# A linear-attention and MLP kernel: chunks 8 to 23 computed by blocks of 64 tokens with the state on the key rows, the powers of w in one table, and a new order

## The chip, the cores and the metric

The kernel runs on one core of a Trainium2 chip. A core has a matrix engine (TensorE, here PE, with its weight loads PEld), a vector engine (DVE), a scalar engine (ACT), GpSimd (POOL) and a queue that issues the DMAs (SP). Each engine takes its instructions in program order and waits for the others by semaphores. The metric is device time in microseconds; the kernel before takes 511.69 us (median of 3 runs, 511.52 to 512.78).

## The reference

Attention with a decaying state for 4 batches, 8 heads, 768 tokens and 48 dimensions per head; its output goes through an MLP (384 to 2048 and back).

```python
for t in range(S):                      # 768 tokens
    cur = einsum('bhd,bhe->bhde', u*k[t], v[t])
    y[t] = einsum('bhd,bhde->bhe', r[t], state + cur)
    state = w * state + einsum('bhd,bhe->bhde', k[t], v[t])
x = y as (3072 tokens, 384)
h = x @ w_in;  sp = log(1 + exp(h))
return (h * erf(sp)) @ w_out
```

## The kernel before

**Chunks.** The 768 tokens are cut into 6 steps of 128; with 4 batches that makes 24 chunks, and chunk g follows chunk g-4 of its own batch. Within a chunk the recurrence is a product: r is scaled by w^i and k by w^-j (steps R and K, tables `wr` and `wk`), A = k^T r is a 128x128 matrix for each head (step A, line 307, matmuls of 48 rows by 64 columns of weights), everything above the diagonal is masked away by a predicated copy into `am` (step P), whose diagonal came from u (steps Q and M). Step Y (line 339) adds two products into one PSUM bank: v with `am`, and the state `sbd` with the scaled r. Step D (line 358) makes the chunk's own contribution to the state, S adds it (line 372) and multiplies by w^128 (line 376). For chunks 8 to 23, half of the A matmuls leave out the 64 columns that the mask drops anyhow, and the predicated copy is made of three pieces. X (lines 379, 382) splits y into a high and a low part, x. D is left out for the last four chunks.

**The MLP.** Four chunks make one block x of 512 tokens. For each of 96 units n (6 blocks by 16 groups of 128 hidden rows) step f (line 405) makes 9 matmuls of 512 columns into `h`, steps a, b, z, c, d, e, g, h, l apply the activation on ACT and DVE (l, the low half `gl`, on DVE or POOL), and step p (line 464) makes 9 matmuls into three accumulators. O copies them out. The weights are split into high and low halves at the start (steps F and C, lines 125 to 137).

**Start and end.** The powers of w are made by doubling on DVE, a square, a reciprocal and a product at a time (lines 175 to 187), from w, with two pairs of tables (`wre`, `wke` for chunks 0 to 3, `wr`, `wk` for the others). Dummy matmuls (W, line 94) fill PE. At the very end step Z counts the heads whose w lies out of a range (a tiny matmul, line 512, and a reduce, line 513); every engine loads the count (line 514) and branches on it (line 596) past a slower version.

**What sets the order.** A string ORDER lists the steps, and each engine gets its instructions in that order; `+` sends a step to POOL, `*` to ACT, none to DVE, and `@` names a PSUM bank. Nothing else schedules them.

```python
L405  nc.tensor.matmul(out=h, lhsT=w[:, f, q, :], rhs=x[:, xi, q, :], ...)   # step f, 9 of them
L464  nc.tensor.matmul(out=acc[e], lhsT=w[:, f, es], rhs=g, ...)             # step p, 9 of them
```

Of the kernel before, what the change touches and what calls it, by code (L numbers as in the profile page):

```python
# [26 lines left out]
P = 128  # L27
C = 128
# [8 lines left out]
V0, K0, R0, AW = 1024, 1472, 1856, 2240  # L37
B0 = AW - 512
# [3 lines left out]
def body(ctx: ExitStack, tc: tile.TileContext, att, early, wcol, u, win, wout, levels, outT):  # L42
# [20 lines left out]
    chunks = {}  # L63


    def load_a(g):
        chunks[g] = (xp if g == 3 else apool).tile([P, AW], F32, tag="x" if g == 3 else "att", name=f"att{g}")
        nc.sync.dma_start(out=chunks[g][:, 0:V0], in_=att[g, :, 0:V0])

    def load_b(g):  # L70
        t = chunks[g]
        if g < 4:
# [68 lines left out]
    pw = fp.tile([PR, 2, NPAIR, C // 2], F32, tag="gh", name="pw")  # L141
    nc.gpsimd.memset(pw[:, 0, :, 0:1], 1.0)
    uq = const.tile([PR, NPAIR, 32], F32, name="uq")
# [31 lines left out]
    nc.vector.tensor_scalar(out=wp[:, 0, 0], in0=wc, scalar1=0.7, scalar2=0.97, op0=ALU.max, op1=ALU.min)  # L175
    for n in range(7):
        m = 1 << n
        nc.vector.tensor_tensor(out=wp[:, n + 1, 0], in0=wp[:, n, 0], in1=wp[:, n, 0], op=ALU.mult)
        nc.vector.reciprocal(out=wp[:, n, 1], in_=wp[:, n, 0])
        if n == 0:  # L180
            nc.vector.tensor_copy(out=pw[:, 1, :, 0], in_=wp[:, 0, 1])
        if n < 6:
            nc.vector.tensor_tensor(out=pw[:, :, :, m:2 * m], in0=pw[:, :, :, 0:m],
                                    in1=wp[:, n, :, :, None].to_broadcast([PR, 2, NPAIR, m]), op=ALU.mult)
    nc.vector.reciprocal(out=wp[:, 7, 1], in_=wp[:, 7, 0])
    for c0, n in ((0, 7), (H, 6)):
        nc.vector.tensor_tensor(out=wke[:, :, c0:c0 + H], in0=pw[:, 1],
                                in1=wp[:, n, 0, :, None].to_broadcast([PR, NPAIR, H]), op=ALU.mult)
        for p in range(NPAIR):
            nc.scalar.mul(out=wre[:, p, c0:c0 + H], in_=pw[:, 0, p], mul=wp[:, n, 1, p:p + 1])  # L190
    for o, i in ((wk, 1), (wr, 0)):
        nc.scalar.copy(out=o[:, :, 0:H], in_=pw[:, i])
        nc.gpsimd.tensor_tensor(out=o[:, :, H:C], in0=pw[:, i],
                                in1=wp[:, 6, i, :, None].to_broadcast([PR, NPAIR, H]), op=ALU.mult)
    for hh in range(2):
        r = slice(64 * hh, 64 * hh + D)
        nc.gpsimd.tensor_tensor(out=uq[r, :, hh], in0=uc[r], in1=wp[r, 0, 0], op=ALU.mult)
# [19 lines left out]

    def prep_k(g, eng):
        t = chunks[g][:PR, 512:V0]
        eng.tensor_tensor(out=t, in0=t, in1=(wke if g < 4 else wk).rearrange("p a c -> p (a c)"), op=ALU.mult)  # L220

    def prep_r(g, eng):
        t = chunks[g][:PR, 0:512]
        eng.tensor_tensor(out=t, in0=t, in1=(wre if g < 4 else wr).rearrange("p a c -> p (a c)"), op=ALU.mult)  # L224

    def prep_n(g, eng):
        t = chunks[g][:, K0:R0]
        eng.tensor_tensor(out=t, in0=t, in1=wkn.rearrange("p a b d -> p (a b d)"), op=ALU.mult)
# [27 lines left out]
    def turn_k(g):  # L256
        tp = bank("h" if g < 4 else "A1", [P, NPAIR, PR], f"kt{g}")
# [11 lines left out]
    def diag_a(t, eng):  # L269
        eng.tensor_tensor(out=t[:, R0:AW], in0=t[:, R0:AW], in1=ub, op=ALU.mult)  # L270

    def diag_b(t, eng):
        eng.tensor_tensor(out=t[:, R0:AW], in0=t[:, R0:AW], in1=t[:, K0:R0], op=ALU.mult)

    def diag_c(t, g):
        q = a2.tile([P, NPAIR, 2], F32, tag="q", name=f"q{g}")
        nc.vector.tensor_reduce(out=q, in_=t[:, R0:AW].rearrange("p (a b d) -> p a b d", b=2, d=D), axis=AX.X,  # L277
# [19 lines left out]
    def a_step(g, tags):  # L297
# [3 lines left out]
        for p in range(NPAIR):  # L301
            for c0, i0 in ((0, 0), (H, H)):
                for hh in range(2):
                    r = slice(64 * hh, 64 * hh + D)
                    jc = c0 if g < 4 else abs(c0 - H * ((hh + p) % 2))
                    i = 0 if g < FULL else i0
                    nc.tensor.matmul(out=ap[hh][jc:jc + H, p, i:C], lhsT=t[r, 512 + p * C + c0:512 + p * C + c0 + H],  # L307
                                     rhs=t[r, p * C + i:(p + 1) * C], start=True, stop=True)
        st_[g]["ap"] = ap

    def predicated(g, am, ap, m, hh):
        if g < FULL:
            nc.vector.copy_predicated(out=by_pair(am), data=by_pair(ap), mask=straight(m) if g < 4 else turned(m, hh))  # L313
            return
        for r, ps, t, c in ((slice(0, P), slice(0, NPAIR), None, slice(H, C)),
                            (slice(0, H), slice(hh, NPAIR, 2), 0, slice(0, H)),
                            (slice(H, P), slice(1 - hh, NPAIR, 2), 1, slice(0, H))):
            if t is None:
                nc.vector.copy_predicated(out=by_pair(am)[:, :, :, c], data=by_pair(ap)[:, :, :, c],
                                          mask=turned(m, hh)[:, :, :, c])  # L320
            else:
                nc.vector.copy_predicated(out=am[r, ps, c], data=ap[r, ps, c],
                                          mask=m[r, t:t + 1, c].to_broadcast([H, NPAIR // 2, H]))
# [38 lines left out]
    def s_views(b, hh):  # L362
        r = slice(64 * hh, 64 * hh + D)
        return r, sbd[r, b, :, D * hh:D * (hh + 1)], wp[r, 7, 0, :, None].to_broadcast([D, NPAIR, D])

    def s_add(g, hh, eng):
        r, sv, w128 = s_views(g % 4, hh)
        ds = st_[g]["ds"]
        if g < 4:
            (nc.scalar.copy if eng is nc.scalar else nc.vector.tensor_copy)(out=sv, in_=ds[r])  # L370
# [135 lines left out]

    def count_bad():

        bad = const.tile([PR, NPAIR], F32, name="bad")
        nc.vector.tensor_tensor(out=bad, in0=wp[:, 0, 0], in1=wc, op=ALU.not_equal)  # L510
# [9 lines left out]
    for i, x in enumerate(words):  # L520
# [11 lines left out]
        elif what == "N" and eng is nc.scalar:  # L532
            copy_k(num)
        elif what in preps:
            preps[what](num, eng)
        elif what == "L":
            (load_a if sub == "a" else load_b)(num)
        elif what == "U":
            load_u()
        elif what == "T":  # L540
            across(wk)
        elif what == "V":
            turn_k(num)
        elif what == "Z":
            rv = count_bad()
        elif what == "Q":
            st_.setdefault(num, {})
            if sub == "a":
                diag_a(chunks[num], eng)
            elif sub == "b":  # L550
                diag_b(chunks[num], eng)
            else:
                st_[num]["q"] = copy_q(num, eng) if num < 4 else diag_c(chunks[num], num)
# [4 lines left out]
        elif what == "H":  # L558
            turn_q(num)
        elif what == "M":  # L560
            st_[num // 10]["am", num % 10] = diag_m(st_[num // 10]["q"], num // 10, num % 10, eng)
        elif what == "A":
            st_.setdefault(num, {})
            a_step(num, [BANKS[c] for c in where or "01"])
        elif what == "P":
# [261 lines left out]
```

## Time and profile before

| what | value |
|---|---|
| time, median of 3 runs | 511.69 us |
| profiled execution, first to last instruction (span) | 508.9 us |
| TensorE clock granted, mean over the span | 0.996 |
| busy: PE, DVE, ACT, POOL | 493.1, 338.1, 403.3, 183.1 us |
| PE h L405 and PE acc L464 on the chain that ended last | 38% and 36% |
| PE y L339, PE A L307, PE ds L358 on it | 6%, 3%, 1% |
| DMA, mean | 93 GB/s |

The profile is of one execution; no device time of that execution is listed beside its span, and the median of the runs lies 2.8 us above it. A matmul's end is modelled, so two matmuls that follow each other overlap in the records: how fast PE goes is read from the starts. A row with xN merges N records; an fp32 matmul leaves two records.

### The profile page before, as it was taken

What the parts mean: (1) busy time and instruction counts of PE and PEld (TensorE: products, weight loads), DVE (VectorE), ACT (ScalarE), POOL (GpSimd) and SP (SyncE); (2) the same over time, 40 slices, a digit from 0 to 9 for tenths busy, and PEclk for the clock granted to TensorE, in tenths of its full rate; (3) what the DMA queues carried; (4) which work ended last, traced back from release to release, by engine and by line L of the source; (5) the groups of instructions that cost most, each with busy time, mean ns of one, the idle gap of its engine ahead of it and who ended that gap; (6) DMA issues with size and microseconds to landing.
All of it is one profiled execution on the core that took longest, in us unless ns stands there. A gap on an engine that the chain in (4) does not pass through costs nothing.

```text
span 508.9 us, 10505 instructions
## 1 busy us (share of the span) xinstructions
PE 493.1 (97%) x4176; PEld 389.5 (77%) x4176; DVE 338.1 (66%) x610; ACT 403.3 (79%) x747; POOL 183.1 (36%) x167
## 2 busy tenths in 40 slices
PE   7789999999999999999999999999999999999994
PEld 3567777877877777787878888787888888878883
DVE  7999999898876956765868644646556453353442
ACT  4788999999997666778776777878778777987982
POOL 6657335433265544625354033513312221202110
PEclk9999999999999999999999999999999999999998
DMA  8656343613605151250131350020120000000001
GB/s 309 222 215 247 123 154 125 216 62 116 243 23 182 64 166 50 90 190 13 51 134 43 105 190 0 7 87 1 63 91 0 1 2 0 33 31 1 0 1 68
DMA packets 14007, 47.34 MB, mean 93 GB/s; under 512 B 1664, under 2 KB 2560, under 8 KB 13952
## 3 DMA queue, kind: packets, MB, share of 16 engines
q1 hardware_dynamic: 13952, 46.61, 26.7%
q8 instruction: 35, 0.57, 0.5%
q14 instruction: 20, 0.16, 0.1%
HBM read 40.31 MB, written 6.29 MB: 92 GB/s over the span
## 4 chain that ended last, share of the span: by engine, by line
PE 86%; DVE 8%; ACT 2%; DMA 1%; issue 1%; POOL 1%; DVEq 0%; ACTq 0%; POOLq 0%
PE h L405 38%; PE acc L464 36%; PE y L339 6%; PE A L307 3%; PE ds L358 1%; DVE s L421 1%; DVE am L313 1%; DMA out_dram<-o 1%; DVE att L220 1%; DMA o<-part 1%; DVE wt L129 1%; DVE gl L448 1%; ACT gh L443 0%; DVE att L224 0%; DVE s L437 0%
## 5 line engine op out<-in xcount | busy, mean ns | idle before, releaser
L405 PE MATMUL h<-x,wih 128*128 128x512 f32 x576 | 183.1, 399 | 1.4 <-DVE s L437 1.0
L448 POOL TENSOR_TENSOR gl<-s,gh 128x512 fp32r<-128x512 f32 x52 | 69.0, 1328 | 213.9 <-ACT gh L443 186.6
L405 PEld LDWEIGHTS h<-x,wih 128*128 128x128 f32 x576 | 106.7, 188 | 28.3 <-DVE s L437 1.9
L464 PE MATMUL acc<-gh,woh 128*128 128x512 f32 x288 | 115.0, 399 | 0.0
L464 PE MATMUL acc<-gl,woh 128*128 128x512 f32 x288 | 114.1, 396 | 0.2 <-DVE gl L448 0.2
L405 PE MATMUL h<-x,wil 128*128 128x512 f32 x288 | 113.7, 395 | 0.0
L464 PE MATMUL acc<-gh,wol 128*128 128x512 f32 x288 | 113.7, 395 | 0.0
L437 DVE SCALAR_TENSOR_TENSOR s<-s,h 128x512 f32<-128x512 f32 x96 | 65.6, 685 | 61.4 <-ACT s L433 61.1
L421 DVE SCALAR_TENSOR_TENSOR s<-s,h 128x512 f32<-128x512 f32 x96 | 65.7, 686 | 59.3 <-ACT s L416 42.4
L425 ACT ACTIVATE s<-s 128x512 f32<-128x512 f32 x96 | 60.2, 628 | 37.3 <-DVE s L421 37.3
L443 ACT CAST gh<-s 128x512 fp32r<-128x512 f32 x96 | 58.7, 614 | 21.6 <-DVE s L437 16.0
L412 ACT ACTIVATE s<-h 128x512 f32<-128x512 f32 x96 | 56.7, 592 | 15.6 <-PE h L405 15.1
L464 PEld LDWEIGHTS acc<-gl,woh 128*128 128x128 f32 x288 | 54.2, 188 | 14.0 <-DVE gl L448 1.5
L464 PEld LDWEIGHTS acc<-gh,woh 128*128 128x128 f32 x288 | 54.1, 188 | 13.4 <-ACT gh L443 0.2
L405 PEld LDWEIGHTS h<-x,wil 128*128 128x128 f32 x288 | 54.1, 188 | 12.9
L464 PEld LDWEIGHTS acc<-gh,wol 128*128 128x128 f32 x288 | 54.2, 188 | 12.7
L416 ACT ACTIVATE s<-s 128x512 f32<-128x512 f32 x96 | 60.4, 632 | 2.1
L433 ACT ACTIVATE s<-s 128x512 f32<-128x512 f32 x96 | 60.3, 629 | 2.1
L429 ACT ACTIVATE s<-s 128x512 f32<-128x512 f32 x96 | 60.4, 629 | 1.9
L448 DVE TENSOR_TENSOR gl<-s,gh 128x512 fp32r<-128x512 f32 x44 | 31.6, 719 | 13.7 <-ACT gh L443 13.1
L290 POOL TENSOR_TENSOR am<-ident,q 128x512 f32<-128x512 f32 x17 | 19.0, 1118 | 25.9 <-DVE q L277 17.6
L339 PE MATMUL y<-am,att 128*32 128x128 f32 x768 | 25.5, 273 | 1.5 <-DVE am L313 1.3
(98 smaller groups left out, 514.0 us busy)
## 6 DMA issues: line engine op xcount, KB each, us to landing
att<-in_att_dram SPq DMA_DIRECT2D x24, 512.0 KB, 4.0
att<-in_att_dram SPq DMA_DIRECT2D x20, 608.0 KB, 5.6
raw<-in_win_dram SPq DMA_DIRECT2D x8, 768.0 KB, 6.4
raw<-in_wout_dram SPq DMA_DIRECT2D x8, 768.0 KB, 4.7
out_dram<-o SPq DMA_DIRECT2D x17, 256.0 KB, 2.2
part<-o SPq DMA_DIRECT2D x6, 256.0 KB, 3.8
o<-part SPq DMA_DIRECT2D x6, 256.0 KB, 4.2
att<-in_early_dram SPq DMA_DIRECT2D x4, 224.0 KB, 8.2
```

The costliest lines, as they stand in the source:

```text
L339: nc.tensor.matmul(out=y[r:r + 32, q, :], lhsT=lhsT, rhs=rhs, start=r not in new, stop=True, skip_group_check=True)
L405: nc.tensor.matmul(out=h, lhsT=w[:, f, q, :], rhs=x[:, xi, q, :], start=k == 0, stop=k == 8)
L412: nc.scalar.activation(out=s1, in_=e["h"], func=AF.Tanh, bias=FB0, scale=FA0)
L416: nc.scalar.activation(out=s1, in_=s1, func=AF.Tanh, bias=FB1, scale=FA1)
L421: nc.vector.scalar_tensor_tensor(out=e["s"], in0=e["s1"], scalar=FG, in1=e["h"], op0=ALU.mult, op1=ALU.add)
L425: nc.scalar.activation(out=s, in_=s, func=AF.Tanh, bias=FB2, scale=FA2)
L429: nc.scalar.activation(out=s, in_=s, func=AF.Square, bias=FB3, scale=FA3)
L433: nc.scalar.activation(out=s, in_=s, func=AF.Square, bias=FB4, scale=FA4)
L437: nc.vector.scalar_tensor_tensor(out=s, in0=s, scalar=FC, in1=ff[n]["h"], op0=ALU.subtract, op1=ALU.mult, reverse0=True)
L443: nc.scalar.copy(out=e["gh"], in_=e["s"])
L448: eng.tensor_tensor(out=e["gl"], in0=e["s"], in1=e["gh"].bitcast(F32), op=ALU.subtract)
L464: nc.tensor.matmul(out=acc[e], lhsT=w[:, f, es], rhs=g, start=first and i == 0, stop=last and i == 2)
```

## The change

Chunks 0 to 7 keep their steps. For chunks 8 to 23 the 128 tokens of a chunk become two halves of 64, each with its own operand tile of 128 rows: 64 rows of v and, on the other 48 rows (where the keys lie in the scaled r), the state that the half starts from. `am` holds the masked A of the half on its token rows and the scaled r on the others, so that one matmul of 32 columns of weights and 64 moving columns does both products of Y. A and the contribution to the state are issued together, head by head. The state now goes through the middle of each chunk: it is added to and multiplied once for each half (step G, then S). A third DMA for each late chunk brings the second half's v into the place where r was. The tables: one tile `pw` of 129 powers, made by seven doublings, and one reciprocal of all of it; chunks 0 to 3 use the same tables. The whole ORDER string is new; step Z stands some steps ahead of the end.

```diff
-    wp = const.tile([PR, 8, 2, NPAIR], F32, name="wp")
-    wr, wk = (const.tile([PR, NPAIR, C], F32, name=n) for n in ("wr", "wk"))
-    wre, wke = (fp.tile([PR, NPAIR, C], F32, tag="s1", name=n) for n in ("wre", "wke"))
...
+    nc.vector.tensor_scalar(out=w1, in0=wc, scalar1=0.7, scalar2=0.97, op0=ALU.max, op1=ALU.min)
     for n in range(7):
         m = 1 << n
...
+        nc.vector.tensor_tensor(out=pw[:, 0, :, m + 1:2 * m + 1], in0=pw[:, 0, :, 1:m + 1],
+                                in1=pw[:, 0, :, m:m + 1].to_broadcast([PR, NPAIR, m]), op=ALU.mult)
+    nc.vector.reciprocal(out=pw[:, 1], in_=pw[:, 0])
...
+    def load_c(g):
+        nc.sync.dma_start(out=chunks[g][:, 0:512], in_=late_att[g - STACKED, :, LW:LW + 512])
...
+    def late_a(g, tags):
...
+        for h in range(NH):
+            for half in range(2):
+                r = HALVES[1 - half]
+                nc.tensor.matmul(out=a[TOKENS[half], h, :], lhsT=kT[r, h, :], rhs=by_half(late_am(g, half))[r, h, :],
+                                 start=True, stop=True)
+            for half in range(2 if g < NCH - 4 else 1):
+                r = TOKENS[half]
+                nc.tensor.matmul(out=d[HALVES[half], h, :], lhsT=t[r, LK + h * D:LK + (h + 1) * D],
+                                 rhs=values(g, half)[r, h * H:h * H + D], start=True, stop=True)
...
+    def late_y(g, tag):
...
+        for n in range(4):
+            for half in range(2):
+                for col in range(4):
+                    q, o, h, c = turns[col][n]
+                    r = STACK[half]
+                    nc.tensor.matmul(out=y[o:o + 32, q, half * H:(half + 1) * H], lhsT=values(g, half)[r, c],
+                                     rhs=by_half(late_am(g, half))[r, h, :], start=o not in new, stop=True,
+                                     skip_group_check=True)
...
+    def middle(g, part, eng):
+        o = kept(g, 1)
+        if part == "a":
+            nc.vector.tensor_tensor(out=o, in0=kept(g, 0), in1=gained(g, 0), op=ALU.add)
+        else:
+            eng.tensor_tensor(out=o, in0=o, in1=decay, op=ALU.mult)
...
-p94x p94y p94z l95 p95x O950a p95y O951a O950b O951b p95z O952a O952b Z0
...
+l94 e95 p93x g95 h95 p94z l95 p94y p94x p95x p95y O950a p95z O952a O951a O952b O951b O950b
```

On DVE at the start of the program, the kernel before makes the powers in small steps (`wp`, `pw`: tables of powers; `att`: a chunk's tile; these rows end with the first product with k).

```order
L178 TENSOR_TENSOR wp<-wp 112x4
L179 RECIPROCAL wp<-wp 112x4
L183 TENSOR_TENSOR pw<-pw,wp 112x8x32
L178 TENSOR_TENSOR wp<-wp 112x4
L179 RECIPROCAL wp<-wp 112x4
L185 RECIPROCAL wp<-wp 112x4
L187 TENSOR_TENSOR wke<-pw,wp 112x4x64 x2
L220 TENSOR_TENSOR att_180<-att_180,wke 112x512
```

The same place on DVE now:

```order
L188 TENSOR_TENSOR pw<-pw 112x4x16
L188 TENSOR_TENSOR pw<-pw 112x4x32
L188 TENSOR_TENSOR pw<-pw 112x4x64
L190 RECIPROCAL pw<-pw 112x516
L338 TENSOR_TENSOR att_143<-att_143,pw 112x512
L342 TENSOR_TENSOR att_143<-att_143,pw 112x512
```

The small reciprocals and the second pair of tables are gone from the front of the first product; one reciprocal of 516 elements stands there instead.

On PE, the rows of chunk 16 (a late one) before: A and, further on, the contribution to the state (ds16) and Y.

```order
L307 MATMUL A16_0_3189<-att16_2840 64x128
L307 MATMUL A16_1_3190<-att16_2840 64x128
L307 MATMUL A16_0_3189<-att16_2840 64x64
L307 MATMUL A16_1_3190<-att16_2840 64x64
...
L358 MATMUL ds16_3302<-att16_2840 48x48 x8
L339 MATMUL y16_3315<-att16_2840,sbd_160 32x128 x12
L339 MATMUL y16_3315<-am16_0_3085,att16_2840 32x128 x2
```

The rows of chunk 16 on PE now (A16d: the contribution to the state; the second half of Y follows its first by four matmuls):

```order
L288 MATMUL A16_3276<-am16_0_3065,att16_2885 64x64
L288 MATMUL A16_3276<-am16_1_3118,att16_2885 64x64
L292 MATMUL A16d_3277<-att16_2885 48x48 x2
...
L314 MATMUL y16_3413<-am16_0_3065,att16_2885 32x64 x4
L314 MATMUL y16_3413<-am16_1_3118,att16_2885 32x64 x4
```

Y has 32 matmuls of 64 columns where it had 28 of 128, and the eight matmuls of ds, now sixteen, stand between those of A.

On ACT at the end of the program before (gh_94 and s2_95: units 94 and 95 of the MLP; fi: the count):

```order
L443 CAST gh_94_5435<-s2_94_5394 128x512
L429 ACTIVATE s2_95_5423<-s2_95_5423 128x512
L433 ACTIVATE s2_95_5423<-s2_95_5423 128x512
L443 CAST gh_95_5442<-s2_95_5423 128x512
L495 COPY o95_0_5458<-acc80_0_5029 128x512
```

The same place on ACT now:

```order
L554 CAST gh_94_5623<-s2_94_5591 128x512
L625 TENSOR_LOAD fi_141
L540 ACTIVATE s2_95_5616<-s2_95_5616 128x512
L544 ACTIVATE s2_95_5616<-s2_95_5616 128x512
L554 CAST gh_95_5650<-s2_95_5616 128x512
```

The load of the count, which stood behind the last copies on every engine, now stands ahead of the activation of the last unit.

## Rows read from the trace of the kernel before

**Rows 1.** The page, part 1: busy time, share of the span, instructions.

```profile
PE 493.1 (97%) x4176; PEld 389.5 (77%) x4176; DVE 338.1 (66%) x610; ACT 403.3 (79%) x747; POOL 183.1 (36%) x167
```

**Rows 2.** Stretches: length, busy PE, PEld, DVE, ACT, POOL (instructions), clock, DMA.

```profile
0.00:33.00 33.00, 25.44 (x462) 16.21 (x462) 29.18 (x65) 21.16 (x65) 20.72 (x30) 1.00 0.67 240
33.00:65.00 32.00, 31.76 (x401) 24.78 (x402) 31.02 (x52) 29.46 (x58) 18.01 (x14) 1.00 0.60 213
155.00:220.00 65.00, 63.79 (x637) 50.51 (x629) 45.43 (x90) 45.49 (x82) 33.68 (x31) 1.00 0.33 108
...
0.00:192.00 192.00, 182.66 (x1819) 140.69 (x1820) 163.08 (x282) 161.04 (x314) 93.56 (x86) 1.00 0.48 165
```

**Rows 3.** Timeline of PE, early chunks: start, length, then engine, line, operation.

```profile
35.76 0.86 PE L339 MATMUL y<-att,sbd 112*32 112x128 f32 x24
...
37.43 1.10 PE L307 MATMUL A<-att 48*64 48x128 f32 x32
38.47 0.73 PE L405 MATMUL h<-x,wih 128*128 128x512 f32 x2
```

**Rows 4.** Timeline of PE where two chunks' Y stand together.

```profile
217.62 0.56 PE L358 MATMUL ds<-att 128*48 128x48 f32 x16
218.11 0.86 PE L339 MATMUL y<-att,sbd 112*32 112x128 f32 x24
...
221.31 0.56 PE L358 MATMUL ds<-att 128*48 128x48 f32 x16
```

**Rows 5.** Timeline of PE, a late chunk's A and what follows it.

```profile
362.08 0.90 PE L307 MATMUL A<-att 48*64 48x128 f32 x32
362.91 0.86 PE L339 MATMUL y<-att,sbd 112*32 112x128 f32 x24
```

**Rows 6.** Groups by line and shape: count, busy us, mean ns, idle before.

```profile
L448 DVE TENSOR_TENSOR gl<-s,gh 128x512 fp32r<-128x512 f32 x44 | 31.6, 719 | 13.7 <-ACT gh L443 13.1
...
L382 DVE TENSOR_TENSOR x<-y,x 128x384 fp32r<-128x384 f32 x24 | 13.0, 550 | 5.7 <-ACT x L379 5.7
...
L372 DVE TENSOR_TENSOR sbd<-sbd,ds 48x192 f32<-48x192 f32 x32 | 11.2, 351 | 5.2 <-PE ds L358 2.9 <-PE y L339 1.8
...
L224 DVE TENSOR_TENSOR att<-att,wr 112x512 f32<-112x512 f32 x10 | 8.7, 891 | 0.0
L94 PE MATMUL dummy<-warm 128*128 128x512 bf16 x26 | 8.3, 467 | 2.4 <-ACT warm L88 2.4
...
L137 DVE TENSOR_TENSOR wil<-wt,wih 128x768 fp32r<-128x768 f32 x5 | 4.8, 960 | 0.9 <-ACT wih L135 0.9
...
L224 DVE TENSOR_TENSOR att<-att,wre 112x512 f32<-112x512 f32 x4 | 2.6, 682 | 0.0
...
L178 DVE TENSOR_TENSOR wp<-wp 112x4 f32<-112x4 f32 x7 | 1.2, 176 | 0.0
L179 DVE RECIPROCAL wp<-wp 112x4 f32<-112x4 f32 x7 | 1.2, 170 | 0.0
```

**Rows 7.** The chain that ended last, from the start to the first unit.

```profile
2.43 0.19 DVE wp L175
...
7.25 1.59 DVE att L220 x2
...
32.25 1.41 DVE x L382 x3
```

**Rows 8.** Lines 514 and 596, the sequencer's part: duration min, median, max.

```profile
L514 PEldq TENSOR_LOAD <-fi x1: 774/774/774, 503.2 to 503.2; - x1
L596 PEldq COMPARE_BRANCH  x2: 95/1892/3690, 504.1 to 504.4; - x2
```

**Rows 9.** Timeline near the end: PE in unit 93, ACT in unit 95, the count.

```profile
496.67 0.40 PE L464 MATMUL acc<-gh,wol 128*128 128x512 f32 x1
496.88 0.63 ACT L429 ACTIVATE s<-s 128x512 f32<-128x512 f32 x1
502.98 0.15 DVE L513 TENSOR_REDUCE fi<-cnt 1x1 int32<-1x4 f32 x1 [0.38 <-PE cnt L512]
```

More of the change, by code (lines that the diff above doesn't have):

```diff
@@ L216, in body, with by_head, paired, values @@
     xts = {}
+    HALVES = [slice(0, D), slice(H, H + D)]
+    TOKENS = [slice(0, H), slice(H, P)]
+    STACK = [slice(0, PR), slice(0, P)]
+    w64 = const.tile([PR, NPAIR, 2], F32, name="w64")
+    def by_head(o):
+        return o.rearrange("r (h c) -> r h c", h=NH)
+    def paired(o, n):
+        return o.rearrange("r (p b c) -> r p b c", p=NPAIR, b=2)[:, :, :, 0:n]
+    def values(g, half):
+        return chunks[g][:, 0:512] if half else chunks[g][:, LV:LW]
+    def kept(g, half):
+        return paired(values(g, half)[HALVES[1 - half]], D)
@@ new lines, in total, with gained, spread @@
+    def total(g):
+        return sbd[HALVES[0], g % 4].rearrange("r p (b d) -> r p b d", b=2)
+    def gained(g, half):
+        return st_[g]["ds"][HALVES[half]].rearrange("r (p b) d -> r p b d", b=2)
+    decay = w64[HALVES[0], :, :, None].to_broadcast([D, NPAIR, 2, D])
+    def spread(step, eng):
+        copy = nc.scalar.copy if eng is nc.scalar else eng.tensor_copy
+        if step < 6:
+            t = (wr, wk)[step // 3]
+            (o, c), i = (((HALVES[1], 1), HALVES[1]), ((HALVES[0], 1), HALVES[1]), ((HALVES[1], 0), HALVES[0]))[step % 3]
+            copy(out=t[o, :, c * H:(c + 1) * H], in_=t[i, :, 0:H])
+        elif step == 6:
+            for hh in range(2):
+                for p in range(2):
+                    o, i = TOKENS[(hh + p + 1) % 2], TOKENS[(hh + p) % 2]
+                    copy(out=wkn[o, p::2, hh, :], in_=wkn[i, p::2, hh, :])
+        else:
+            for hh in range(2):
+                copy(out=w64[HALVES[0], :, hh], in_=wr[HALVES[hh], :, H])
@@ new lines, in by_half, with late_am, late_r @@
+    def by_half(o):
+        return o.rearrange("p a (b c) -> p (a b) c", b=2)
+    def late_am(g, half):
+        s = st_.setdefault(g, {})
+        if ("am", half) not in s:
+            s["am", half] = a2.tile([P, NPAIR, C], F32, tag=f"am{half}", name=f"am{g}_{half}")
+        return s["am", half]
+    def late_r(g, half, eng):
+        r = (slice(H, PR), slice(0, H))[half]
+        eng.tensor_tensor(out=late_am(g, half)[r], in0=chunks[g][r, 0:512].rearrange("p (a c) -> p a c", c=C),
+                          in1=wr[r], op=ALU.mult)
@@ new lines, in late_p @@
+    def late_p(g, half):
+        r = TOKENS[half]
+        nc.vector.copy_predicated(out=by_half(late_am(g, half))[r], data=st_[g]["A"][r],
+                                  mask=mask[r, half, 0:H].bitcast(U32)[:, None, :].to_broadcast([H, NH, H]))
+    def late_y(g, tag):
+        y = st_[g]["y"] = bank(tag, [P, NQ, C], f"y{g}")
+        turns = [[], [], [], []]
+        for k in range(12):
+            p, i = k // 3, k % 3
+            for hh in ((0,), (0, 1), (1,))[i]:
+                c = P * p + (0, 32 + 16 * hh, 80)[i]
+                turns[k % 4].append((k // 4, 32 * (k % 4), 2 * p + hh, slice(c, c + 32)))
+        new = set()
+        for n in range(4):
[6 more added lines that the diff above has]
+                                     skip_group_check=True)
+                    new.add(o)
@@ L533, in body @@
             copy_k(num)
+        elif what == "R" and num >= STACKED:
+            late_r(num, "ab".index(sub), eng)
         elif what in preps:
@@ L536, in body @@
         elif what == "L":
-            (load_a if sub == "a" else load_b)(num)
+            dict(a=load_a, b=load_b, c=load_c)[sub](num)
         elif what == "U":
             load_u()
+        elif what == "T" and num:
+            spread(num - 1, eng)
         elif what == "T":
+            nc.vector.tensor_tensor(out=bad, in0=w1, in1=wc, op=ALU.not_equal)
             across(wk)
         elif what == "V":
-            turn_k(num)
+            turn_k(num, BANKS[where or "h"])
         elif what == "Z":
@@ L559, in body @@
             turn_q(num)
+        elif what == "M" and num >= 10 * STACKED:
+            late_m(num // 10, num % 10, eng)
         elif what == "M":
             st_[num // 10]["am", num % 10] = diag_m(st_[num // 10]["q"], num // 10, num % 10, eng)
+        elif what == "A" and num >= STACKED:
+            late_a(num, [BANKS[c] for c in where or "01"])
         elif what == "A":
@@ L564, in body @@
             a_step(num, [BANKS[c] for c in where or "01"])
+        elif what == "P" and num >= 10 * STACKED:
+            late_p(num // 10, num % 10)
         elif what == "P":
             predicated(num // 10, st_[num // 10]["am", num % 10], st_[num // 10]["ap"][num % 10], mask.bitcast(U32), num % 10)
+        elif what == "Y" and num >= STACKED:
+            late_y(num, BANKS[where or "h"])
         elif what == "Y":
@@ L572, in body @@
             st_.setdefault(num, {})["ds"] = ds_product(chunks[num], BANKS[where] if where else "h" if num < 4 else "A1", f"ds{num}")
+        elif what == "G":
+            middle(num, sub, eng)
+        elif what == "S" and (num >= STACKED or num >= STACKED - 4 and sub in "cd"):
+            passed(num, sub, eng)
         elif what == "S":
```

297 lines of the change are left out of this document (160 added, 137 removed).

## Prediction

> **What bounds the kernel now.** I read the busy shares first, then the stretches, then the chain of waits and the timeline of PE. PE is busy for 97% of the span, ACT for 79%, DVE for 66%, POOL for 36% [rows 1]; the reader is to see that no average speaks against PE as the bound, and that two engines are not far behind. By stretches [rows 2] it is sharper. Up to 33 us PE is not the bound: DVE is busy for 29.2 of 33 us, PE for 25.4 with its dummies. From 33 us on PE loses 0.24 us in 32, and between 155 and 220 us 1.2 us in 65. So the time is the start, up to the first MLP unit, plus all that PE has to stream, plus few waits. But DVE was busy for 31.0 of the 32 us from 33 to 65, and for 163.1 of the first 192: there it just keeps up. The chain of waits agrees: from the start to 33.7 us it runs mostly over DVE, from the setting of w at 2.43 by the first product with k at 7.25 to the last low halves of x at 32.25 [rows 7].
>
> The timeline gives the price of attention on PE. An early Y lasts from 35.76 to 37.43, 1.67 us, an early A from there to 38.47, 1.04 us [rows 3]; two Y in a row last from 218.11 to 221.31, 3.20 us, and a ds 0.49 us in front of them [rows 4]; a late A lasts from 362.08 to 362.91, 0.83 us [rows 5].
>
> **The change part by part.**
>
> *PE, chunks 8 to 23.* Removed: sixteen A (0.83 each, 13.3), twelve ds (0.49, 5.9), ten single Y (1.67) and three pairs (3.20), 26.3 us: 45.5 us together. What is added has no row, so I take the old rows apart. Y leaves 56 records on four column groups, 14 rounds; the second Y of a pair adds 1.53 us, so a round of 128 columns is 0.109 us, and 0.14 us of a Y is fixed. An early A has 8 rounds on four tiles, 0.87 us, and 0.17 us fixed. A late A has four of them narrowed to 64 columns: 0.83 less 0.17 less 0.44 leaves 0.22, or 0.055 for a narrow round. Columns decide, not the number of records. A ds, 48 columns, has 8 rounds in 0.49 us, 0.06 us each with its fixed part. I take 0.058 for a round of 64. The new Y has 64 records, 16 rounds: 0.93 and 0.14, 1.07 us. The 32 records of the new A lie on two of four tiles, 16 rounds: 0.93 and 0.17, 1.10 us; the sixteen products for the state stand between them on the other two tiles and are hidden there. That is 2.17 us for a chunk, 34.7 us for sixteen: **-10.8 us**. If a narrow round cost as much as a wide one and ds were not hidden, a chunk would take 1.88, 1.91 and 0.49, 4.28 us, +23 us in all; at 0.055, -12. The late A is the nearest row, and it is the same kind of instruction, so I stay near its end.
>
> *PE, small items.* Two dummies behind the first unit, 0.32 us each (8.3 us by 26 [rows 6]), and 34 stretches of attention instead of 31, each with about 0.16 us of the fixed part above: **+1.1 us** (0 to +2).
>
> *The start.* The table took from 2.43 to 7.25, 4.8 us [rows 7]. Now: the setting (0.19), seven doublings, the smallest like the 0.176 of L178, the largest below the 0.68 of 112x512, together about 1.9 us, and one reciprocal of 516 elements. With four elements a reciprocal took 170 ns, a product 176 [rows 6], so they do not differ there; a product of 512 elements took 682 [rows 6], about 1 ns for an element. If a reciprocal differed by a tenth at four elements, 17 ns, 516 of them would take 2.2 us more. So 0.7 to 2.9 us; I take 0.7, the row of the same size. The first product with k can then start at 5.2 instead of 7.25. Further on to x DVE loses two products with r, one diagonal, and products that go to POOL, and gains two e-products, six products for the state and one split of weights; by the rows that is about 1 us less. But the chunks arrive by DMA, two thirds busy in the mean over these 33 us [rows 2], and DVE will wait for them a little more. **-2 us** (-3.5 to +0.5).
>
> [...]
>
> *DVE and POOL, up to the 31st unit of the MLP.* The state goes through 10 sums and as many products of 48x384 by then, where the kernel before had half the size: a 48x192 sum is 0.35 us and a read of 384 elements from PSUM 0.55 [rows 6]; DVE's part grows by about 5.5 us. Five more splits at 0.96, four more low halves at 0.72, four more products with r at 0.68 [rows 6] are 10.4 us. Fewer products with k, N and Q, and the late predicated copy in one piece instead of three, give back about 4, the start 2: some +10 us, so 173 us within some 185, 93% instead of 85%. Later in the program it evens out. ACT's work grows by 3 us in all. DVE did 97% from 33 to 65 us while PE lost 0.24 us [rows 2], so the cover can hold; if it does not, PE stalls. I charge **+2 us** (0 to +8).
>
> POOL gets some 30 us more work. The same product of DVE took 682 ns at the start and 891 later on [rows 6], so company costs something. [...]
>
> *The end.* The load of the count now stands on PE, ACT, DVE and POOL ahead of the last unit's work. PE's sixth matmul of unit 93 starts at 496.67; the count's matmul would start at 496.95, the reduce 0.22 us later, 0.15 long, the load 0.77 [rows 8, 9]: free at 498.15. ACT's next step starts at 496.88 now [rows 9]; it is on the chain to the end: **+1.3 us** (0 to +1.7). PE then branches (3.69 us [rows 8]) without the count just ahead of it, but the last four output DMAs are issued one after the other behind the last copy; I set these against each other (-1 to +0.5).
>
> Queues: the third DMA of a late chunk waits on SP until both products with r are done, and what stands behind it on SP are loads of later chunks and outputs; in the order it stands some units ahead of its reader, so nothing is charged. A delay there would show as the fourth rival.
>
> **Sum.** -10.8 + 1.1 - 2 + 2 + 1.3 = -8.4: a span of 500.5 us for 508.9. The median of the runs lies 2.8 us above the span; so **503.3 us**.
>
> **The rivals.**
> 1. *The reciprocal is slow.* It holds up the whole start, since every product waits for the table. [...] For it: it is the one instruction with no row of its size. Against it: equal rows at four elements.
> 2. *DVE cannot keep up, and the kernel is slower.* Place: the first 185 us; price: 173 us of work at a share s of the time. It decides against the change where s falls below 0.89: 173/0.88 is 197 us, 12 us beyond the 185, less the 2 charged: 513 to 514; at today's 85% it would be over 519. For it: three engines above 90% at once, each in order. Against it: the 97% from 33 to 65 us.
> 3. *PE pays by the record.* A Y record takes 0.030 us (1.67 by 56); 128 records instead of some 100 would be 61 us instead of 45.5, about 530 us. The narrowed A speaks against it.
> 4. *The gain turns into waits for the state.* Y now waits for a sum on DVE and a product, half of the time on POOL, behind A. Half a microsecond late in each of sixteen chunks is 8 us: 511.5, no change. Against it: 18 to 72 MLP matmuls lie between an A and its Y.
> 5. *Everything fits*: start -3, no stalls, nothing at the end: 499.
>
> **How the numbers follow.** Forecast 0.45, its own range 500 to 506; slow reciprocal 0.22; DVE 0.11; by the record 0.03; waits for the state 0.07; all fits 0.12. A measurement of this kernel tells 0.3%, 1.5 us, from no change. Faster: 0.45 + 0.22 + 0.12 = 0.79; same 0.07; slower 0.14. The range that holds 8 in 10 goes from 497 (0.055 for a round, all fits) to 513 (where the second rival begins).
>
> **What would show it.** In the changed profile: an A with its ds near 1.1 us from start to start and a Y near 1.07; the reciprocal's row near 0.7 us and the first product with k near 5.2; the first MLP matmul near 31; PE's idle time between there and 190 us some 2 us above today's; ACT idle about 1.3 us at the load of the count. The forecast is wrong if A or Y stays above 1.5 us, if the first MLP matmul comes after 34 us, or if PE waits for DVE over 8 us in the first 190.

## The result, and the profile after

The changed kernel is slower: 518.32 us in the median of 4 runs (516.15 to 518.88) against 511.61 (511.32 to 512.78), a ratio of 1.011 (95% interval 1.0084 to 1.0136). 503.3 was forecast, and the range ended at 513. The profiled execution has a span of 516.5 us for 508.9.

The page's first part, the line that answers to [rows 1]: busy time, share of the span, instructions of each engine.

```profile
PE 491.3 (95%) x4575; PEld 381.5 (74%) x4575; DVE 364.0 (70%) x537; ACT 399.4 (77%) x761; POOL 216.7 (42%) x195
```

DVE has 26 us more work in fewer instructions, POOL 34 us more. The stretches show where that falls. First the changed kernel (length, busy PE, PEld, DVE, ACT, POOL with instructions, clock, DMA share, GB/s); the first two and the last answer to [rows 2]:

```profile
0.00:33.00 33.00, 28.10 (x398) 16.10 (x400) 28.05 (x45) 19.45 (x60) 15.43 (x26) 0.90 0.64 235
33.00:65.00 32.00, 30.74 (x442) 23.84 (x441) 31.05 (x47) 27.72 (x59) 20.05 (x16) 1.00 0.56 194
65.00:104.00 39.00, 35.87 (x237) 26.59 (x236) 37.05 (x55) 35.17 (x64) 16.27 (x13) 1.00 0.42 142
104.00:166.00 62.00, 58.55 (x539) 45.56 (x540) 58.41 (x82) 52.38 (x91) 29.36 (x25) 1.00 0.49 162
0.00:192.00 192.00, 179.12 (x1989) 132.75 (x1993) 178.52 (x261) 156.47 (x318) 96.34 (x93) 0.98 0.49 168
```

and the kernel before in the two middle stretches, which its rows above don't show:

```profile
65.00:104.00 39.00, 38.66 (x243) 31.00 (x242) 35.53 (x51) 37.97 (x68) 16.49 (x13) 1.00 0.44 148
104.00:166.00 62.00, 62.00 (x460) 49.19 (x459) 48.37 (x81) 55.24 (x96) 26.24 (x21) 1.00 0.39 133
```

Between 65 and 166 us PE loses 6.6 us to idleness where it lost 0.3. DVE is busy for 95% of these 101 us where it was for 83%, and before for 91% up to 104 already. Over the first 192 us DVE now stands at 93%, the share that the prediction worked out (173 us in 185), but the work behind that share is not the work that it worked out. Counted up to one place in both kernels, the start of the 31st MLP unit (181.4 us before, 193.0 now), first the kernel before and then the changed one:

```profile
0.00:181.38 181.38, 172.06 (x1712) 132.16 (x1712) 156.82 (x267) 154.72 (x302) 88.02 (x81) 1.00 0.47 162
0.00:193.00 193.00, 179.79 (x2014) 133.22 (x2014) 178.79 (x262) 157.44 (x320) 96.34 (x93) 0.98 0.49 167
```

DVE has 22.0 us more work to do by then, where some +10 was forecast (ACT's +2.7 is near the 3 forecast). The share came out at 93% because the time grew as well, by 11.6 us. So both were wrong: how much work is added, and that PE would pay only 2 us for it.

The new attention work came out as forecast. On PE's timeline (start, length, engine, line, operation) a new Y goes from 173.86 to 174.91 and an A with the products for the state from there to 175.99: 1.05 and 1.08 us, against 1.67, 0.83 and 0.49 in [rows 3 to 5].

```profile
173.86 1.11 PE L314 MATMUL y<-am,att 112*32 112x64 f32 x64
174.91 0.27 PE L288 MATMUL A<-am,att 48*64 48x64 f32 x2
...
175.99 0.50 PE L516 MATMUL h<-x,wih 128*128 128x512 f32 x1
```

I read the two traces by PE's starts alone: each stretch of attention at the shortest that its form shows, each MLP matmul at 0.233 us (eighteen of them start from 157.80 to 161.76 in the changed kernel), and what is left as waiting. The terms are good to about a microsecond, since they depend on how the stretches are cut. The last matmul is that of an MLP unit in the changed kernel and that of the count in the kernel before, 0.6 us behind the MLP's last.

| term (us) | predicted | before | after | difference |
|---|---|---|---|---|
| first MLP matmul | -2 | 33.03 | 35.55 | +2.5 |
| work from there to the last matmul | -9.7 | 460.5 | 449.0 | -11.5 |
| waits in it up to 65 us | | 2.1 | 3.7 | +1.6 |
| waits from 65 to 166 us | +2 (with the row above, up to some 190 us) | 1.5 | 10.2 | +8.7 |
| waits from 166 to 300 us | | 3.7 | 5.5 | +1.8 |
| waits behind 300 us (the count) | +1.3 | 1.9 | 4.0 | +2.1 |
| behind the last matmul | 0 | 6.0 | 8.7 | +2.7 |
| span | -8.4 | 508.9 | 516.5 | +7.6 |

(The stretches' waits are rounded one by one, so the column adds to 7.9. The first row is one trace against one: in the four other traces of kernels that begin like the changed one the first MLP matmul came at 35.7 to 37.3, and at 34.5 in the other trace that begins like the kernel before.)

The start. The timeline of DVE, and of PE at the first unit, in the changed kernel; [rows 7] had the first product with k at 7.25:

```profile
2.42 0.18 DVE L185 TENSOR_SCALAR pw<-wu 112x4 f32<-112x4 f32 x1 [1.21 <-DMA wu<-in_wcol_dram]
2.63 2.07 DVE L188 TENSOR_TENSOR pw<-pw 112x4 f32<-112x4 f32 x7
...
4.81 3.38 DVE L190 RECIPROCAL pw<-pw 112x516 f32<-112x516 f32 x1
...
8.22 1.42 DVE L338 TENSOR_TENSOR att<-att,pw 112x512 f32<-112x512 f32 x1
...
35.55 0.82 PE L516 MATMUL h<-x,wih 128*128 128x512 f32 x2
```

The reciprocal takes 3.38 us where 0.7 was taken; the first product with k comes 1.0 us later, not 2.0 earlier.

How a wait arises in the middle is seen at 150 us. Timeline, several engines; in brackets what was idle before, and who ended it:

```profile
147.48 2.10 POOL L559 TENSOR_TENSOR gl<-s,gh 128x512 fp32r<-128x512 f32 x1 [1.24 <-issue]
...
148.46 1.92 DVE L144 SCALAR_TENSOR_TENSOR wt<-raw,wt 128x768 int32<-128x768 int32 x1
...
150.42 0.84 ACT L147 CAST woh<-wt 128x768 fp32r<-128x768 f32 x1 [2.55 <-DVE wt L144]
...
151.29 0.97 DVE L149 TENSOR_TENSOR wol<-wt,woh 128x768 fp32r<-128x768 f32 x1 [0.90 <-ACT woh L147]
...
152.29 0.69 DVE L532 SCALAR_TENSOR_TENSOR s<-s,h 128x512 f32<-128x512 f32 x1
...
152.89 0.55 DVE L493 TENSOR_TENSOR x<-y,x 128x384 fp32r<-128x384 f32 x1
...
153.50 0.73 PE L516 MATMUL h<-x,wih 128*128 128x512 f32 x2 [1.75 <-DVE x L493]
```

A step of the weights' decoding that takes 0.95 us alone takes 1.92 beside POOL's product (the step just ahead of it, at 147.47, ran beside the same product in 0.96, so company doesn't cost every time). ACT waits 2.55 us for it and DVE 0.90 for ACT, because the low half stands next in DVE's order. The step of the MLP and the low half of x stand behind it, and PE idles 1.75 us for x. Nothing here is long by itself; three engines in fixed order pass the delay on.

### The profile page after: what moved, and what is told of

It reads as the page before. It is cut to its first block, busy times and chain, and to the rows that moved or that the text cites. A ratio compares the mean times of both kernels' runs of the same rounds, so it can differ in the third digit from the quotient of the medians.

```text
span 516.5 us, 11307 instructions
## 1 busy us (share of the span) xinstructions
PE 491.3 (95%) x4575; PEld 381.5 (74%) x4575; DVE 364.0 (70%) x537; ACT 399.4 (77%) x761; POOL 216.7 (42%) x195
## 4 chain that ended last, share of the span: by engine, by line
PE 52%; DVE 4%; ACT 3%; DMA 2%; issue 1%; POOL 1%; SPq 0%; ACTq 0%; POOLq 0%
PE acc L575 24%; PE h L516 24%; PE y L314 2%; DMA att<-in_late_att_dram 2%; PE A L288 1%; DVE s L548 1%; ACT s L544 1%; DVE att L324 1%; ACT s L540 1%; ACT gh L554 1%; DVE am L267 1%; DVE s L532 1%; ACT s L527 0%; ACT s L536 0%; DVE am L297 0%
## 5 line engine op out<-in xcount | busy, mean ns | idle before, releaser
L559 POOL TENSOR_TENSOR gl<-s,gh 128x512 fp32r<-128x512 f32 x56 | 77.3, 1381 | 169.0 <-ACT gh L554 150.6
L559 DVE TENSOR_TENSOR gl<-s,gh 128x512 fp32r<-128x512 f32 x40 | 29.6, 741 | 16.2 <-ACT gh L554 15.1
L267 POOL TENSOR_TENSOR am<-att,pw 48x512 f32<-48x512 f32 (+1 forms) x17 | 22.6, 1328 | 7.3 <-PE y L314 6.5
L277 POOL TENSOR_TENSOR am<-ident,q 64x512 f32<-64x512 f32 x18 | 21.4, 1188 | 7.1 <-DVE q L400 6.6
```

Source lines behind the costliest of these rows:

```text
L267: eng.tensor_tensor(out=late_am(g, half)[r], in0=chunks[g][r, 0:512].rearrange("p (a c) -> p a c", c=C), in1=wr[r], op=ALU.mult)
L559: eng.tensor_tensor(out=e["gl"], in0=e["s"], in1=e["gh"].bitcast(F32), op=ALU.subtract)
```

## The experiments

The experiments test one theory and its rivals. The theory: the gain on PE is there, and three things eat it: VectorE's load up to about the 22nd MLP unit, the reciprocal ahead of everything, and the new end. A rival puts PE's waits down to the new order, whatever VectorE's load. All were timed against the kernel before on the same chip (511.0 to 511.6). The differences below are to the changed kernel's 518.32, which was timed apart from them, or, for the variants of the kernel before, to its time on the same chip.

**joint.** The reciprocal of 4 elements, and doublings of w and 1/w side by side.

```diff
+    nc.vector.reciprocal(out=pw[:, 1, :, 1], in_=w1)
     for n in range(7):
-        nc.vector.tensor_tensor(out=pw[:, 0, :, m + 1:2 * m + 1], ...
+        nc.vector.tensor_tensor(out=pw[:, :, :, m + 1:2 * m + 1], ...
-    nc.vector.reciprocal(out=pw[:, 1], in_=pw[:, 0])
```

> The changed kernel with one edit: the reciprocal is taken of w alone (4 elements), and the seven doublings run over w and 1/w side by side, so the RECIPROCAL of 516 elements (3.38 us in the changed kernel's trace) is gone and the doublings grow by 508 elements in all. Theory 1 (VectorE has no slack from the start to about the 22nd MLP unit, so work taken off it there comes back whole): table about 2.6 us shorter, first MLP matmul about 33 us instead of 35.5, the whole about 2.6 us faster than the changed kernel's 518.3: 515.7. Rival (the start waits for the chunks' transfers and the stalls later are waits for results that the new order puts too close): first MLP matmul moves by under 1 us and the time by under 1 us.

513.86 us, 4.5 us less than the changed kernel, and the first unit 3.6 us earlier. DVE's timeline, and PE's:

```profile
2.64 0.18 DVE L186 RECIPROCAL pw<-pw 112x4 f32<-112x4 f32 x1
2.85 2.52 DVE L189 TENSOR_TENSOR pw<-pw 112x8 f32<-112x8 f32 x7
5.41 0.69 DVE L338 TENSOR_TENSOR att<-att,pw 112x512 f32<-112x512 f32 x1
...
31.94 0.73 PE L516 MATMUL h<-x,wih 128*128 128x512 f32 x2
```

The product with k starts at 5.41, 2.8 us earlier; DVE is busy for 27.8 us ahead of the first unit where it was for 30.6. So 4.5 us by the medians is more than the step's work (the two profiled spans, 513.4 and 516.5, differ by 3.1). From the 4th to the 25th unit the lead is only 1.8 us, since PE's waits up to 65 us rise from 3.7 to 6.4: a part of the gained start is waited away behind VectorE.

**warm16.** `WARM = 16` for 10, to see whether the rest of that is the clock.

> The changed kernel with 16 dummies at the start instead of 10. In its trace TensorE ran out of dummies at 6.6 us and stood still to 8.3, and the granted clock of 8 to 16 us was 0.55 to 0.59; with the table done at 6.8 us (the kernel joint) it was 1.00 and the first MLP unit came 3.6 us earlier, for 2.6 us of work less. Theory A (the clock is the rest): clock 1.00 there, first MLP unit 0.5 to 1.2 us earlier, time 517 to 518. Rival (the 16 dummies end at 9 us, behind the table at 8.2, and hold up the first products): no gain or up to 0.8 us later.

517.67 us. The granted clock between 8 and 16 us was 1.00 for 0.57, and the first unit came at 35.2 for 35.55. Neither the 0.65 us by the medians nor the 0.3 us at the first unit is clear of the spread: in the changed kernel and the four that begin exactly like it the first unit came between 35.5 and 37.3. So no cost of the lower clock at the start was seen, and why joint gains more than 2.8 us at the first unit is left open.

**splits.** `C10f C01f C13f C15f C16f` go to GpSimd (`+`), `C12f+` to VectorE.

> The changed kernel with one edit: the low halves of the weights of groups C10, C01, C13, C15 and C16 go back from VectorE to GpSimd and that of C12 to VectorE, as in the kernel before (8 on GpSimd, 8 on VectorE). Theory 1 (VectorE has no slack up to the 22nd unit): five by 0.96, less what GpSimd's five by 1.8 us stretch on VectorE; 3 to 5 us faster than the changed kernel, 513 to 515. Rival (GpSimd's reads stretch VectorE's work by as much as they take off it): VectorE's mean for the decoding steps rises and the time moves by under 1 us, or is slower.

523.79 us, 5.5 slower: the theory missed, and the rival, which had allowed for a slower kernel, named a part of the cause. Up to the 25th unit DVE was busy for 150.6 us where it was for 151.8, though four splits fewer (five moved, one came back) would be 3.8 us; the rest of its work had grown by the difference. The rival's own sign, higher means of the decoding steps, is mixed from 33 to 166 us: L141 rose from 0.95 to 1.03 us, L144 fell from 1.28 to 1.17. And these 150.6 us took 170.3 us for 163.2. DVE had become idle for 8.3 us more, 2.7 of them ahead of the first unit: the waits of DVE from 33 to 200 us (us in total, times, longest) show for what:

```profile
DVE q L400 <- POOL att L396: 4.3, 2, 2.5
DVE wt L139 <- ACT wt L137: 2.9, 3, 2.3
```

The first was 0.4 in the changed kernel, the second 0.2. Work on POOL is slower (in the changed kernel a split takes 1.83 to 1.84 us there, and 0.95 in the median on DVE) and what DVE needs stands behind it. Behind a wait of 3.2 us for x the granted clock of PE was 0.50 from 159.2 to 162.5 (0.91 in the mean from 155 to 160 and 0.87 from 160 to 170, where the changed kernel had 1.00); in dup_before, below, MLP matmuls at 0.50 started every 0.43 us instead of 0.233, so a part of the 5.5 us is the clock. "VectorE has no slack" doesn't mean that moving its work helps: here it cost 5.5 us.

**dup_after, dup_before.** Five low halves computed twice (`C11f C11f`, and C03f, C05f, C04f, C06f), in either kernel.

> The changed kernel with the low halves of the weights of groups C11, C03, C05, C04 and C06 computed twice on VectorE, one after the other (the second writes the same numbers): 4.8 us more work on VectorE between the 4th and the 18th unit, nothing else. Theory 1: no slack, so +4 to +5 us: 522.5 to 523.5. Rival (the stalls are waits for results, VectorE itself has room): under +2 us.

> The kernel before with the same five low halves computed twice on VectorE, 4.8 us more work between the 4th and the 19th unit. If the kernel before had no slack on VectorE either (its trace has VectorE at 69 us of work in the 67 us from the first unit to the 15th, though 85% on the mean of the first 192 us), it is +3 to +5 us: 514.6 to 516.6. If the 85% was slack that could be used, as the prediction took it, under +1 us.

525.63 us (+7.3) and 520.25 (+9.2): 4.8 us of VectorE's work cost more than themselves in both. In the traces either span grew by 9.6 us, of which 1.8 and 1.5 came ahead of the first unit, where nothing had been changed; 7.8 and 8.1 are left. So the kernel before had no room there either; its 85% was the mean over a stretch that is full at first and freer behind 104 us. (The 69 us of work in 67 us of the expectation are lengths of rows, which overlap on DVE, as two products with r of 0.68 us that take 1.28 from 10.68 do; as busy time it is 63.4 us in 66.9, or 95%.) Why dup_before's rest is above 4.8 stands in part in its trace, first by stretches, then on PE:

```profile
62.00:66.00 4.00, 2.23 (x18) 1.55 (x20) 3.84 (x6) 3.71 (x9) 0.00 (x0) 1.00 0.05 20
66.00:68.00 2.00, 1.51 (x34) 0.90 (x26) 1.97 (x3) 1.96 (x4) 0.96 (x1) 0.89 0.88 280
68.00:70.00 2.00, 0.82 (x2) 0.73 (x3) 2.00 (x3) 0.84 (x1) 2.00 (x2) 0.50 0.97 391
70.00:74.00 4.00, 4.00 (x10) 3.07 (x10) 3.85 (x6) 2.09 (x5) 0.03 (x1) 0.50 0.06 21
```

```profile
65.74 1.10 PE L307 MATMUL A<-att 48*64 48x128 f32 x32 [1.77 <-issue]
...
69.18 0.79 PE L405 MATMUL h<-x,wil 128*128 128x512 f32 x1 [1.68 <-DVE wil L137]
...
72.76 0.63 PE L464 MATMUL acc<-gl,woh 128*128 128x512 f32 x1
73.19 0.63 PE L464 MATMUL acc<-gh,wol 128*128 128x512 f32 x1
```

PE waited 1.8 us up to 65.74, worked up to 67.5 and then waited 1.7 us more. The granted clock was still 1.00 up to 66 and 0.50 from 68 on, so it fell about when the second wait began and not behind it. Matmuls started every 0.43 us instead of 0.233 until 74. A wait alone doesn't always do this: behind the changed kernel's 1.75 us at 153.5 the clock stayed at 1.00.

**no_c_after, no_c_before.** The step L141 (L129 before) left out, 15 us of VectorE's work; the weights lose their lowest three bits.

> The changed kernel without the step of the weights' decoding that puts in the lowest three bits (L141, 16 times 0.95 us on VectorE, all up to the 22nd unit; the weights lose these bits, nothing else is left out): 15 us less on VectorE. Theory 1 (the gain on TensorE is there, and VectorE's load up to the 22nd unit eats it): TensorE's waits between 33 and 166 us, some 8 us more than before, go; 518.3 falls to 506 to 510. Rival (the waits come from the new order, which puts a result too close to its reader whatever VectorE's load is): 514 to 518.

> The kernel before without the same step, 15 us less on VectorE. Its waits on TensorE between 33 and 166 us were 3 to 4 us, so by theory 1 it gains 3 to 5 us at most (506 to 508.5) and the changed kernel without the step is level with it or faster by up to 3 us. By the rival the changed kernel stays some 7 us behind.

509.45 us (-8.9) and 508.47 (-3.1). In the changed kernel PE is full again where it idled:

```profile
65.00:104.00 39.00, 38.99 (x255) 30.50 (x254) 36.16 (x51) 37.33 (x67) 17.80 (x16) 1.00 0.43 154
104.00:166.00 62.00, 60.92 (x554) 48.09 (x553) 54.89 (x83) 54.23 (x96) 28.30 (x25) 1.00 0.43 148
```

The order is the same but for the words taken out, and the waits from 65 to 166 us fall from 10.2 to 3.4, so the order by itself isn't the cause. (Without the step DVE is busy for 136.6 us up to the 25th unit, where it was for 151.8 with it and for 128.9 in the kernel before.) From the first MLP matmul to the end of the last matmul, the changed kernel takes 472.3 us and 462.1 without the step; the one before 469.9 and 469.6. Without that load the change is worth 7.5 us on this stretch, and the start and the end take it back. Leaving the step out also shortens the chain from a weight's load to its use; the runs don't tell that apart from the load.

**tail_both, out_order.** The end as before; and only its outputs.

```diff
-p95x p95y O950a p95z O952a O951a O952b O951b O950b
+p95x O950a p95y O951a O950b O951b p95z O952a O952b
```

(tail_both also puts `Z0` last again.)

> The changed kernel with its end as in the kernel before: the count and its load behind all units, the last outputs in the old order, each sent as soon as it is copied. From the last p matmul's start to the end of the span the changed kernel takes 9.0 us, the one before 6.8; the count's stall is about 1.3 us more. Theory (both are on the path): 518.3 less 2 to 3.5 us. Rival (the branch and the last transfer end last either way): under 1 us.

> The changed kernel with only the last outputs in the old order (each sent as soon as it is copied), the count still ahead of the last unit. tail_both gave 3.6 us. If the count's place is the larger part of it, 517; if the order of the outputs is, 515 to 515.5. From the trace the order should be: the last two transfers are issued 1.5 and 3 us behind the last copy.

514.73 (-3.6) and 515.80 (-2.5, its runs 514.41 to 518.34). The runs of the two overlap, so these medians alone don't divide the gain. The traces do: from the start of the last MLP matmul to the end of the span it is 8.3 to 9.5 us in the seven traces with the new order of the outputs and 6.9 to 7.6 in the four with the old one, about 1.4 us on the mean. The count stands between two MLP matmuls that start 1.29 us apart (500.95 and 502.24) where 0.233 is usual, so it costs about 1.1 us. Here are PE at the count and SP at the end in the changed kernel, then SP in tail_both:

```profile
500.95 0.40 PE L575 MATMUL acc<-gh,wol 128*128 128x512 f32 x1
501.28 0.19 PE L623 MATMUL cnt<-bad,mask 112*1 112x4 f32 x2
502.24 0.47 PE L575 MATMUL acc<-gh,woh 128*128 128x512 f32 x1 [0.78 <-DVE fi L624]
...
508.31 0.81 SPq L585 DMA_DIRECT2D out_dram<-o  x2
509.22 1.96 SPq L587 DMA_DIRECT2D out_dram<-o  x2
```

```profile
504.92 1.14 SPq L587 DMA_DIRECT2D out_dram<-o  x2
506.15 0.90 SPq L585 DMA_DIRECT2D out_dram<-o  x2
```

With the two halves of the last output first in the queue, the two that were copied earlier wait behind them: SP's last issue ends 2.6 us behind the last copy (511.2 behind 508.6) where it ends 0.7 us behind it in tail_both (507.05 behind 506.35), and the last transfer lands 5.4 us behind it where it lands 3.9.

**contend.** Five products on GpSimd that nobody reads, at the places of the five doubled low halves.

```diff
+            nc.gpsimd.tensor_tensor(out=scr, in0=ident..., in1=mask..., op=ALU.mult)
```

> The changed kernel with five more products on GpSimd (128x384, both inputs in SBUF, into a tile that nobody reads), ahead of the low halves of C11, C03, C05, C04 and C06: about 5 us more GpSimd work, none more on VectorE. GpSimd is idle half of that time. Theory of the port (GpSimd's reads stretch VectorE's products and shifts with all operands in SBUF): VectorE's busy time up to the 24th unit rises by 2 us or more, time +2 to +5. Rival (GpSimd's slack is free): time within 1 us of 518.3.

The port in the theory's name was the author's assumption: no trace here shows one. What the run tests is whether VectorE's rows get longer.

521.17 us, +2.9, with nothing added on VectorE. DVE was busy for 154.7 us up to the 25th unit where it was for 151.8. In the traces 1.0 of these 2.9 us, and 1.0 of the span's 2.9, came ahead of the first unit, where nothing had been changed. By line and shape from 33 to 166 us (busy us, mean ns), the changed kernel and then contend:

```profile
L144 DVE SCALAR_TENSOR_TENSOR wt<-raw,wt 128x768 int32<-128x768 int32 x14 | 17.9, 1275 | 0.4
L141 DVE SCALAR_TENSOR_TENSOR wt<-raw,wt 128x768 int32<-128x768 int32 x14 | 13.3, 953 | 0.2
L139 DVE TENSOR_SCALAR wt<-wt 128x768 int32<-128x768 int32 x14 | 10.0, 714 | 0.3 <-ACT wt L137 0.2
L149 DVE TENSOR_TENSOR wil<-wt,wih 128x768 fp32r<-128x768 f32 x6 | 6.4, 1066 | 0.0
L434 DVE COPY_PREDICATED am<-mask,A 128x512 f32<-128x512 uint32 x8 | 5.8, 737 | 0.0
```

```profile
L144 DVE SCALAR_TENSOR_TENSOR wt<-raw,wt 128x768 int32<-128x768 int32 x14 | 16.3, 1164 | 0.4
L141 DVE SCALAR_TENSOR_TENSOR wt<-raw,wt 128x768 int32<-128x768 int32 x14 | 14.7, 1052 | 0.2
L139 DVE TENSOR_SCALAR wt<-wt 128x768 int32<-128x768 int32 x14 | 11.2, 802 | 0.7 <-ACT wt L137 0.6
L149 DVE TENSOR_TENSOR wil<-wt,wih 128x768 fp32r<-128x768 f32 x6 | 7.7, 1279 | 0.0
L434 DVE COPY_PREDICATED am<-mask,A 128x512 f32<-128x512 uint32 x8 | 5.8, 741 | 0.0
```

Of the four groups that read SBUF alone three were stretched and one, L144, was shortened by as much as L141 was stretched; the copy that reads PSUM stayed as it was. The single rows show that the form alone doesn't decide it. Of the changed kernel's sixteen L144 eleven took 0.94 to 0.96 us, and five, each beside work on POOL, 1.65 to 2.05; five others beside work on POOL were not stretched. So a busier GpSimd goes with some 2 us more of VectorE's time here, though it was idle half of that stretch, and which rows are stretched changes from kernel to kernel.

**best, best_no_c.** joint and tail_both together, and that without the step L141.

> The changed kernel with both edits that were faster by themselves: the reciprocal of w alone with doublings over w and 1/w (4.5 us by itself) and the end of the kernel before (3.6 us by itself). If the two add, 510.2, about level with the kernel before (511.6) or faster by up to 0.4%. Rival: VectorE's load after the first unit takes back what the start gives (joint led by 3.6 us at the first unit and by 1.8 us from the 4th to the 25th), 512 to 513.

> The same without the step of the weights' decoding that puts in the lowest three bits (the weights lose these bits, as in no_c_after): all three losses named (start, end, VectorE's load up to the 22nd unit) taken away together. If these three are all that stood between the prediction's 10 us on TensorE and the time, 509.45 - 4.5 - 3.6 = 501.4, 7 us faster than the kernel before without that step (508.5), and the prediction's 503.3 less the 2 us charged for stalls. Rival (something else is lost on the way): 505 or more.

best: 510.66 us (12 runs, 508.43 to 512.75), a ratio of 0.9982 (0.9966 to 0.9998) to the kernel before: level with it or a few tenths of a percent faster, and the first version with all bits that isn't slower. best_no_c: 499.64, 1.8 us under the sum of the three parts; it isn't a version to use, since the weights lose bits, but it shows that the three losses add up. The like-for-like comparison is with no_c_before, the kernel before without that step: 8.8 us faster, where the change was forecast at -8.4.

## Why the prediction was wrong, by its own steps

- *PE, chunks 8 to 23:* right. -10.8 was forecast; sixteen times 1.08, twelve times 1.04 and two pairs of 1.95 are 33.7 us for 45.5: -11.8. Columns decided, not records (64 records of 64 columns in 1.04, 56 of 128 in 1.67), and the products for the state lay hidden in A (1.08 with them, where 1.10 was forecast for an A by itself).
- *Small items:* +1.1 forecast, +0.3 found.
- *The start:* the term that was mis-sized is the reciprocal, 0.7 taken and 3.38 measured, outside the 0.7 to 2.9 that the prediction gave it. Four elements couldn't show it: on a line through the two rows, an estimate, an element takes (3377 - 170) / 512 or 6.3 ns, and four of them only 25 of the 170 ns. So the first rival came true, and joint prices it at 4.5 us with what follows from it. Its chance of 0.22, counted among the faster outcomes, was the author's estimate: no run had shown a reciprocal of that size. The first MLP matmul came at 35.55, past the 34 that the prediction named as a sign of being wrong.
- *DVE and POOL up to the 31st unit:* the step that failed, in its size and in its price. The work added on DVE by the 31st unit was put at +10 us and measured at +22.0; that the share is 93% as forecast is luck, since the time grew with the work. Two of the terms came out by the lengths of their rows (the state +6.8 for 5.5, the splits +4.6 for 4.8); the 6 us that were to be given back did not come, with the masked copies at 19.2 us for 17.9, and the weights' decoding, which the change doesn't touch, took 3.2 us more. The price was +2 against +8.7 between 65 and 166 us and +1.6 ahead of that. The cover that the prediction named, 97% from 33 to 65 us with PE losing 0.24 us [rows 2], was one stretch, not a rule, and the mean of 85% hid that the stretches up to 104 us were full and the free time lay behind it. Second, a load's length isn't all: at 93% DVE still waits for ACT and POOL in its order, and such waits reach PE (1.75 us for x at 153.5). The second rival had this place and mechanism; but it looked for a share below 0.89 with 173 us of work, and what came was 178.8 us of work at 0.93, and its price of 513 lacked the start and the end.
- *Company of POOL:* the sum has no term for it, and that was too little, as far as one trace shows. Five more products went with 2.9 us (contend), about 2 of them behind the first unit. The 891 ns that the prediction used are a mean of unlike rows: six of those ten products ran with no work of POOL beside them in 0.68 to 0.69 us, four beside it in 0.92 to 1.79. How much of the changed kernel's own +8.7 is that, and how much new work, no run here separates.
- *The end:* +1.3 for the count was about right (1.1 in the trace). Setting the branch against the four outputs at nothing was wrong: the outputs' order costs about 1.4 us by the traces (2.5 by the medians). The prediction saw that they are issued one after the other, and not that two were held back behind the last.

Nothing came of the third rival (PE by the record), and of the fourth nothing was seen in the changed kernel's trace: a late Y waited 0.35 us at 133.8, for its masked A (L297), and another 0.32 us at 192.7 for nothing that the trace names; none is shown waiting for the state.

## What to carry to other kernels

An engine's mean busy share is no cover: cut the stretch until the shares stop changing, and count work where it is due, not where the mean has room. Where three engines in fixed order each stand at 90% or above, as PE, DVE and ACT did here from 65 to 104 us in both kernels, price added work on one at its length or more (here 4.8 us cost 7.3 and 9.2) and don't expect that moving it to a slower engine helps (here it cost 5.5). A share that comes out as forecast proves nothing while the time moves too; compare the work up to the same place. Price an operation by a row of its own size, and when none exists, let the range, not the hope, hold the upper bound.

## What the runs showed of the hardware

- A RECIPROCAL of 516 elements a partition took 3.38 us, where one of 4 took 0.17 to 0.18; on a line through the two that is an estimate of 6.3 ns an element.
- Half the columns nearly halved the time of a small matmul: the old Y took 1.67 us for 56 records of 128 columns, the new one 1.04 to 1.05 for 64 records of 64, both on four column groups: 0.030 and 0.016 us a record.
- Some steps of VectorE with all operands in SBUF took longer beside work of GpSimd: a decoding step (L144) 0.95 us alone and 1.65 to 2.05 in five of ten rows beside such work, a product with r of the kernel before (L224 with `wr`) 0.68 to 0.69 in six rows alone and 0.92 to 1.79 in four beside it.
- In dup_before the granted clock fell from 1.00 to 0.50 as the second of two waits of 1.8 and 1.7 us began and stayed there for some 6 us, in which MLP matmuls started every 0.43 us instead of 0.233: those waits cost more than their length. A lower clock at the start (0.57 between 8 and 16 us) showed no cost clear of the spread (warm16).
